# K cache loaded as whole 32 KB rows with four heads side by side, and one ring of three tiles for wq, K, V and wo

## The chip, the cores and the metric

The kernel runs on one core of one Trainium2 chip. A core has TensorE (PE, matmuls; its weight loads are shown apart as PEld), VectorE (DVE), ScalarE (ACT), GpSimd (POOL) and SyncE (SP), which here only issues transfers. Sixteen DMA engines move data between the chip's main memory (DRAM in the names) and the on-chip memory SBUF, which has 128 partitions; matmuls write to PSUM. The metric is the device time of one execution in microseconds (us).

## The reference

One token passes through an attention branch and a gated feed-forward branch; a sigmoid gate mixes both. All arrays are bf16, and of the cache of 65536 positions only the last 4096 are used.

```python
# D=512, Hq=32 query heads, Hkv=8 cached heads, Dh=128, W=4096, F=1792
q = (x @ wq).reshape(B, Sq, Hq, Dh).transpose(0, 2, 1, 3)      # wq: 512 x 4096
k = repeat(k_cache[:, :, Sk - W:, :], 4, axis=1)
v = repeat(v_cache[:, :, Sk - W:, :], 4, axis=1)
p = softmax(einsum("bhqd,bhkd->bhqk", q, k) * Dh ** -0.5)
a = einsum("bhqk,bhkd->bhqd", p, v).reshape(B, Sq, Hq * Dh) @ wo   # wo: 4096 x 512
b = (sigmoid(x @ w_gate) * (x @ w_up)) @ w_down
g = sigmoid((x * gate_w).sum(-1))
out = g * a + (1 - g) * b
```

## The kernel before, in words

**Loads.** All large loads are issued on SP, in this order: wq (4 MB, line 76), K as two loads of four heads each (4 MB each, lines 83 to 86), w_gate and w_up (1.75 MB each, lines 88 to 91), V as one load of heads 0 to 3, one of heads 4 and 5, and one each of heads 6 and 7 (lines 96 to 107) with w_down in two halves between them, and wo in six pieces (lines 109 to 112, bounds in `WO_SPLIT`). In the K and V loads partition p gets 32 consecutive positions of each head, which is one run of 8 KB per head and partition (`load_blocks`, line 78).

**Buffers.** A tile pool hands out a fixed number of buffers per tag; a new tile waits until the tile that had the buffer is no longer used. Pool `big` has one buffer of 32 KB per partition: wq, and after it wo. Pool `blk` has two of 32 KB: the two K tiles `kn`, and after them the two V tiles `vv`. Pool `ktp` has four of 8 KB: `q_sb`, `qtT`, then the transposed K tiles `kT`. So V's first load waits on SP until heads 0 to 3 of K have been transposed, V's second until heads 4 to 7 have been, and wo until wq has been read.

**The query (lines 153 to 173).** For each k of 4, eight matmuls (four chunks c of wq by two halves of 512 columns) make 1024 columns of x @ wq, equal in all partitions; ACT copies them to `q_sb`, DVE transposes them in 32 x 32 blocks of 4-byte words into `qtT`, and after the fourth k eight DVE copies scatter the query into `qbig`, whose slices are the stationary operands of the scores.

**The scores S (lines 176 to 188).** For each head g, DVE transposes the head's K tile in 32 x 32 blocks of 4-byte words, that is, of bf16 pairs (line 180). A pair holds two of the head's dimensions, so the dimension index is split into dhi (which half), a part that lies on the partitions, and t (which of the pair). Four pairs (dhi, t) by two halves of the positions give 8 matmuls of 512 columns per head, all of which accumulate in the two PSUM banks of `S_ps` (line 185). Neighbouring columns of the moving operand lie 2 elements apart, which is 4 bytes:

```python
        k_v = kT[:].rearrange("p (kb dhi s t) -> p kb dhi s t", kb=KB, dhi=2, s=32)
                                     rhs=k_v[:, hb * 16:(hb + 1) * 16, dhi, :, t],
```

**From S to the output.** DVE takes the row maxima of S (`pm`, line 192), PE and DVE bring them together per head (lines 194 to 199), ACT computes exp with the row sums (line 205), and DVE transposes the result into `eT` (line 207). PE meanwhile makes the gate and up products `gu_ps` (line 215), and DVE and ACT turn them into `hT` (lines 221 to 231). Then come the row sums per head (`rb_ps`, line 237), the products with V (`pv_ps`, line 267, two groups of four heads), their selection and scaling (lines 272 to 279), a transpose to `oY` (lines 283 to 287), and two matmuls of one row per 128 rows of w_down and of wo (`add_row`, line 248), all summed in `a_ps`. DVE and ACT copy one half of it each, and two transfers write the output.

**What sets the order.** Each engine runs its instructions in one order, fixed when the kernel is built; across engines, they wait for one another on semaphores. A transfer on SP that waits for a buffer holds back the transfers behind it in the order of issue.

Of the kernel before, what the change touches and what calls it, by code (L numbers as in the profile page):

```python
# [9 lines left out]
AF = mybir.ActivationFunctionType  # L10
ALU = mybir.AluOpType
AX = mybir.AxisListType
BF16 = mybir.dt.bfloat16
F32 = mybir.dt.float32
# [3 lines left out]
def kernel(  # L18
# [14 lines left out]
    nc = tc.nc  # L33

    P = 128
    D = A_x.shape[-1]
    DC = D // P
    Hkv = A_k_cache.shape[1]
    Sk = A_k_cache.shape[2]
    DH = A_k_cache.shape[3]  # L40
    HQ = A_wq.shape[1] // DH
    REP = HQ // Hkv
    W = min(4096, max(256, Sk // 4))
    KB = W // P
    SBASE = Sk - W
# [8 lines left out]
    scale = float(DH) ** -0.5  # L54
# [1 line left out]
    NJ_A = NJ // 2  # L56

    const = ctx.enter_context(tc.tile_pool(name="const", bufs=1))
    big = ctx.enter_context(tc.tile_pool(name="big", bufs=1))
    blk = ctx.enter_context(tc.tile_pool(name="blk", bufs=2))  # L60
    w14 = ctx.enter_context(tc.tile_pool(name="w14", bufs=3))
    ktp = ctx.enter_context(tc.tile_pool(name="ktp", bufs=4))
    work = ctx.enter_context(tc.tile_pool(name="work", bufs=1))
    ps_big = ctx.enter_context(tc.tile_pool(name="ps_big", bufs=2, space=bass.MemoryType.PSUM))
    ps_S = ctx.enter_context(tc.tile_pool(name="ps_S", bufs=1, space=bass.MemoryType.PSUM))
# [7 lines left out]
    dq = nc.sync  # L73
    wq_sb = big.tile([P, DC, HQ * DH], BF16, name="wq_sb", tag="big")
    wq_v = A_wq.rearrange("(p c) n -> p c n", c=DC)
    dq.dma_start(wq_sb[:], wq_v)

    def load_blocks(t, cache, g0, n, at=0):
        dq.dma_start(t[:, at:at + n, :, :],
                     cache[0, g0:g0 + n, SBASE:SBASE + W, :].rearrange("g (p kb) d -> p g kb d", kb=KB))  # L80

    kn = []
    for i in range(2):
        t = blk.tile([P, 4, KB, P], BF16, name="kn", tag="blk")
        load_blocks(t, A_k_cache, 4 * i, 4)
        kn += [t[:, j] for j in range(4)]

    wg_sb = w14.tile([P, DC, F], BF16, name="wg_sb", tag="w14")
    dq.dma_start(wg_sb[:], B_w_gate.rearrange("(p c) f -> p c f", c=DC))
# [5 lines left out]

    vv = []
    for i in range(2):
        t = blk.tile([P, 4, KB, P], BF16, name="vv", tag="blk")
        vv += [t[:, j] for j in range(4)]
        if i == 0:  # L100
            load_blocks(t, A_v_cache, 0, 4)
        else:
            load_blocks(t, A_v_cache, 4, 2)
            load_blocks(t, A_v_cache, 6, 1, at=2)
            dq.dma_start(wd_sb[:, 0:NJ_A, :], wd_v[:, 0:NJ_A, :])
            load_blocks(t, A_v_cache, 7, 1, at=3)
            dq.dma_start(wd_sb[:, NJ_A:NJ, :], wd_v[:, NJ_A:NJ, :])
# [24 lines left out]
    for c in range(DC):  # L132
        nc.tensor.matmul(xt_ps[:, c:c + 1], lhsT=xr[:, 0, c:D:DC], rhs=ident[0:1, 0:1],  # L133
                         start=True, stop=True, skip_group_check=True)
# [15 lines left out]
    nc.vector.tensor_scalar(gg[:, 1:2], gg[:, 0:1], -1.0, 1.0, op0=ALU.mult, op1=ALU.add)  # L150


    q_sb = ktp.tile([P, HQ * DH], BF16, name="q_sb", tag="kt")
    qtT = ktp.tile([P, HQ * DH], BF16, name="qtT", tag="kt")
    for k in range(4):
        q_ps = ps_big.tile([P, 2, 512], F32, name="q_ps", tag="b")
        for c in range(DC):
            for hb in range(2):
                n0 = k * 1024 + hb * 512
                nc.tensor.matmul(q_ps[:, hb, :], lhsT=xT[:, c:c + 1].to_broadcast([P, P]),  # L160
                                 rhs=wq_sb[:, c, n0:n0 + 512], start=(c == 0), stop=(c == DC - 1))
        nc.scalar.copy(q_sb[:, k * 1024:(k + 1) * 1024], q_ps[:].rearrange("p a b -> p (a b)"))  # L162
        nc.vector.transpose(qtT[:].bitcast(F32)[:, k * 512:(k + 1) * 512],  # L163
                            q_sb[:].bitcast(F32)[:, k * 512:(k + 1) * 512])

    q_src = qtT[:].rearrange("p (g hh dhi r t) -> p g hh dhi r t", g=Hkv, hh=REP, dhi=2, r=32)
    q_dst = qbig[:].rearrange("p (g y) -> p g y", y=2 * GS)[:, :, 0:4 * P] \
        .rearrange("p g (dhi c t) -> p g c dhi t", dhi=2, t=2)
    for qd in range(4):
# [3 lines left out]
    q_st = qbig[:, 0:Hkv * 4 * P].rearrange("p (g dhi c t) -> p g dhi c t", g=Hkv, dhi=2, t=2)  # L173


    S_ps = ps_S.tile([P, 2, 512], F32, name="S_ps", tag="S")
    S_f = S_ps[:].rearrange("p a b -> p (a b)")
    for g in range(Hkv):
        kT = ktp.tile([P, KB * P], BF16, name="kT", tag="kt")
        nc.vector.transpose(kT[:].bitcast(F32), kn[g].rearrange("p k d -> p (k d)").bitcast(F32))  # L180
        k_v = kT[:].rearrange("p (kb dhi s t) -> p kb dhi s t", kb=KB, dhi=2, s=32)
        for dhi in range(2):
            for t in range(2):
                for hb in range(2):
                    nc.tensor.matmul(S_ps[:, hb, :], lhsT=q_st[:, g, dhi, :, t],  # L185
                                     rhs=k_v[:, hb * 16:(hb + 1) * 16, dhi, :, t],
                                     start=(g == 0 and dhi == 0 and t == 0),
                                     stop=(g == Hkv - 1 and dhi == 1 and t == 1))


    pm = work.tile([P, 1], F32, name="pm")
# [8 lines left out]
                     start=True, stop=True)  # L200
    nb = work.tile([P, 1], F32, name="nb")
    nc.scalar.mul(nb[:], mb_ps[:], -scale)
    e_sb = work.tile([P, W // 4], BF16, name="e_sb")
    rs = work.tile([P, 1], F32, name="rs")
    nc.scalar.activation(e_sb[:], S_f, AF.Exp, bias=nb[:], scale=scale, accum_out=rs[:])
    eT = work.tile([P, Hkv, KB, REP], BF16, name="eT")
    nc.vector.transpose(eT[:].rearrange("p g k h -> p k g h"),
                        e_sb[:].rearrange("p (k g h) -> p k g h", g=Hkv, h=REP))
# [3 lines left out]
    for c in range(DC):  # L212
        for j in range(4):
            for w, wsb in enumerate((wg_sb, wu_sb)):
                nc.tensor.matmul(gu_ps[32 * j:32 * j + 32, w, 0:FQ],  # L215
                                 lhsT=xT[:, c:c + 1].to_broadcast([P, 32]),
                                 rhs=wsb[:, c, j * FQ:(j + 1) * FQ], start=(c == 0), stop=(c == DC - 1))
# [39 lines left out]
    for b in range(2):  # L257
        last = b == 1
        pv_ps = ps_big.tile([P, 4, P], F32, name="pv_ps", tag="b")
        for gq in range(4):  # L260
            g = 4 * b + gq
            if g == Hkv - 1:
                down(0, NJ_A)
            for m in range(KB // 4):
# [3 lines left out]
                                 lhsT=eT[:, g, 4 * m:4 * m + wj, :].rearrange("p k h -> p (k h)"),  # L268
                                 rhs=vv[g][:, 4 * m:4 * m + 4, :],
                                 start=(m == 0), stop=(m == KB // 4 - 1), skip_group_check=True)  # L270
# [5 lines left out]
        for j in range(4):  # L276
            nc.tensor.matmul(o_ps[:], lhsT=pv_sb[:, j, :], rhs=sel_v[:, j, :, :],  # L277
                             start=(j == 0), stop=(j == 3))
# [49 lines left out]
```

## Time and profile before

| What | Value |
|---|---|
| Median of 3 runs | 81.83 us (81.78 to 82.42) |
| Profiled execution: its time | 81.94 us |
| Profiled execution: span from the first to the last instruction | 80.2 us |
| Moved by DMA | 30.71 MB in 3738 packets, mean 383 GB/s over the span |
| PE, PEld, DVE, ACT, POOL busy | 48.7, 22.8, 35.1, 8.8, 5.0 us |
| Matmuls of S (line 185), 64 | 17.0 us busy, from 27.84 to 45.1 us |
| Transposes of K (line 180), 8 | 17.7 us busy, from 25.48 to 43.14 us |
| wq lands | 13.07 us |
| Last wo matmul ends | 77.44 us |

Times in the profile count from the start of the span. The span is shorter than the time of the execution by what lies around it. Each of the 40 digits in a row of slices is the busy share of 2.0 us in tenths; PEclk is the clock that TensorE was granted, in tenths of full speed. A line of the timeline gives the start, the length, the engine and line, what is written from what, how many such instructions were merged, and in brackets the idle time before and what ended it. Durations of matmuls overlap, so their pace is read from the starts of neighbours or from a group's length over its count.

### The profile page before, as it was taken

The numbers are of one execution on the slowest core, as the hardware profiler recorded it, in microseconds if no ns is written. First come the engines' busy times: TensorE is split into PE (matmuls) and PEld (weight loads), VectorE is DVE, ScalarE is ACT, GpSimd is POOL, SyncE is SP. The second block draws the span as 40 slices with busy tenths as digits, with TensorE's granted clock in tenths as the row PEclk, the third lists the DMA queues.
The fourth block names the chain that finished last, engine by engine and source line by source line (L and its number), as shares of the span: only waits on it lengthen the run. The fifth ranks groups of instructions, "written<-read, shape, count | busy, mean of one in ns | idle before, by whom it ended". The sixth has DMA issues, their size and how long they took to land.

```text
span 80.2 us, 774 instructions
## 1 busy us (share of the span) xinstructions
PE 48.7 (61%) x313; PEld 22.8 (28%) x313; DVE 35.1 (44%) x43; ACT 8.8 (11%) x13; POOL 5.0 (6%) x10
## 2 busy tenths in 40 slices
PE   0010204999800199999998970007999699678560
PEld 0000201344200032344443430004333545356330
DVE  0000720014359999999995449998000000020020
ACT  2400000055630000000000035000000200200010
POOL 7970000000000000000000000000000000000000
PEclk9999999999999655699999999555558999999999
DMA  7679988999999999999999999999999999999400
GB/s 180 262 343 524 425 360 372 442 425 425 425 425 417 433 409 445 419 451 422 422 397 437 401 433 413 429 413 425 413 418 436 416 426 417 425 409 399 182 8 1
DMA packets 3738, 30.71 MB, mean 383 GB/s; under 512 B 276, under 2 KB 408, under 8 KB 920
## 3 DMA queue, kind: packets, MB, share of 16 engines
q1 hardware_dynamic: 3730, 30.67, 92.3%
q8 instruction: 2, 0.03, 0.2%
q10 hardware_dynamic: 6, 0.00, 0.0%
HBM read 30.67 MB, written 0.00 MB: 383 GB/s over the span
## 4 chain that ended last, share of the span: by engine, by line
DMA 57%; DVE 23%; PE 12%; issue 3%; ACT 1%; DVEq 0%
DMA wo_sb<-in_A_wo_dram 23%; DVE kT L180 20%; DMA vv<-in_A_v_cache_dram 18%; DMA wq_sb<-in_A_wq_dram 15%; PE q_ps L160 11%; DVE qbig L172 2%; PE a_ps L248 2%; ACT q_sb L162 1%; DVE qtT L163 1%; DVE res L294 1%; DVEq L180 0%; DVEq L172 0%
## 5 line engine op out<-in xcount | busy, mean ns | idle before, releaser
L185 PE MATMUL S_ps<-kT,qbig 128*128 128x512 bf16 x64 | 17.0, 429 | 6.4 <-DVE kT L180 6.4
L180 DVE STREAM_TRANSPOSE kT<-kn 128x2048 f32<-128x2048 f32 x8 | 17.7, 2274 | 0.0
L267 PE MATMUL pv_ps<-vv,eT 128*16 128x512 bf16 (+1 forms) x64 | 12.0, 465 | 0.0
L185 PEld LDWEIGHTS <-qbig 128*128 128x128 bf16 x64 | 6.8, 106 | 16.5 <-issue 6.6
L160 PE MATMUL q_ps<-wq_sb,xT 128*128 128x512 bf16 x32 | 8.6, 437 | 3.2 <-DMA wq_sb<-in_A_wq_dram 3.2
L163 DVE STREAM_TRANSPOSE qtT<-q_sb 128x512 f32<-128x512 f32 x4 | 2.8, 711 | 10.0 <-ACT q_sb L162 10.0
L279 DVE TENSOR_TENSOR oT<-o_ps,rb 128x16 bf16<-128x16 f32 x2 | 0.3, 174 | 14.6 <-PE o_ps L277 14.6
L267 PEld LDWEIGHTS <-eT 128*16 128x16 bf16 (+1 forms) x64 | 4.5, 104 | 6.4 <-issue 3.6
L160 PEld LDWEIGHTS <-xT 128*128 128x128 bf16 x32 | 3.5, 109 | 7.9 <-issue 5.3
L162 ACT CAST q_sb<-q_ps 128x1024 bf16<-128x1024 f32 x4 | 4.0, 1012 | 8.6 <-PE q_ps L160 8.6
L248 PE MATMUL a_ps<-wo_sb,oY 128*1 128x256 bf16 x64 | 4.2, 272 | 1.2 <-DMA wo_sb<-in_A_wo_dram 1.2
L237 PE MATMUL rb_ps<-lsel,ones_f 128*128 128x32 f32 x2 | 0.6, 398 | 6.9 <-DVE lsel L235 6.9
L141 DVE TENSOR_TENSOR gpr<-xr 1x512 f32<-1x512 bf16 x1 | 0.7, 679 | 7.9 <-DMA xr<-in_gate_w_dram 7.9
L126 POOL MEMSET qbig<- 128x4160 bf16 x1 | 3.6, 3564 | 0.0
L248 PEld LDWEIGHTS <-oY 128*1 128x1 bf16 x64 | 2.9, 83 | 2.5 <-issue 1.7
L133 PE MATMUL xt_ps<-ident,xr 1*128 1x1 bf16 x4 | 0.3, 165 | 5.2 <-POOL ident L118 5.2
L272 ACT COPY pv_sb<-pv_ps 128x512 f32<-128x512 f32 x2 | 1.2, 585 | 19.1 <-PE pv_ps L267 19.1
L221 ACT ACTIVATE sge<-gu_ps 128x448 f32<-128x448 f32 x1 | 0.5, 543 | 24.6 <-PE gu_ps L215 24.6
L294 DVE CAST res<-a_ps 1x256 bf16<-1x256 f32 x1 | 0.4, 412 | 5.9 <-PE a_ps L248 5.9
L224 DVE RECIPROCAL sg<-sge 128x448 f32<-128x448 f32 x1 | 3.0, 2954 | 0.0
L144 PE MATMUL z_ps<-gsum,ones_f 1*128 1x1 f32 x2 | 0.6, 358 | 3.9 <-DVE gsum L142 3.9
L277 PE MATMUL o_ps<-identf,pv_sb 128*128 128x16 f32 x16 | 2.1, 265 | 1.4 <-ACT pv_sb L272 1.4
(49 smaller groups left out, 28.2 us busy)
## 6 DMA issues: line engine op xcount, KB each, us to landing
kn<-in_A_k_cache_dram SPq DMA_DIRECT2D x2, 4096.0 KB
wq_sb<-in_A_wq_dram SPq DMA_DIRECT2D x1, 4096.0 KB, 12.3
vv<-in_A_v_cache_dram SPq DMA_DIRECT2D x1, 4096.0 KB, 18.1
wo_sb<-in_A_wo_dram SPq DMA_DIRECT2D x3, 1024.0 KB, 22.7
vv<-in_A_v_cache_dram SPq DMA_DIRECT2D x1, 2048.0 KB
vv<-in_A_v_cache_dram SPq DMA_DIRECT2D x2, 1024.0 KB, 16.3
wg_sb<-in_B_w_gate_dram SPq DMA_DIRECT2D x1, 1792.0 KB, 35.0
wu_sb<-in_B_w_up_dram SPq DMA_DIRECT2D x1, 1792.0 KB, 32.5
```

Of the source, the lines that this page charges most:

```text
L126: nc.gpsimd.memset(qbig[:], 0.0)
L160: nc.tensor.matmul(q_ps[:, hb, :], lhsT=xT[:, c:c + 1].to_broadcast([P, P]), rhs=wq_sb[:, c, n0:n0 + 512], start=(c == 0), stop=(c == DC - 1))
L162: nc.scalar.copy(q_sb[:, k * 1024:(k + 1) * 1024], q_ps[:].rearrange("p a b -> p (a b)"))
L163: nc.vector.transpose(qtT[:].bitcast(F32)[:, k * 512:(k + 1) * 512], q_sb[:].bitcast(F32)[:, k * 512:(k + 1) * 512])
L172: nc.vector.tensor_copy(q_dst[rows, :, 32 * qd:32 * qd + REP, :, t], q_src[rows, :, :, :, 0, t])
L180: nc.vector.transpose(kT[:].bitcast(F32), kn[g].rearrange("p k d -> p (k d)").bitcast(F32))
L185: nc.tensor.matmul(S_ps[:, hb, :], lhsT=q_st[:, g, dhi, :, t], rhs=k_v[:, hb * 16:(hb + 1) * 16, dhi, :, t], start=(g == 0 and dhi == 0 an ...
L224: nc.vector.reciprocal(sg[:], sge[:])
L248: nc.tensor.matmul(a_ps[32 * i:32 * i + 1, i, 0:HN], lhsT=lhsT, rhs=rhs[:, i * HN:(i + 1) * HN], start=start, stop=stop)
L267: nc.tensor.matmul(pv_ps[32 * gq:32 * gq + mm, :, :], lhsT=eT[:, g, 4 * m:4 * m + wj, :].rearrange("p k h -> p (k h)"), rhs=vv[g][:, 4 * m ...
L277: nc.tensor.matmul(o_ps[:], lhsT=pv_sb[:, j, :], rhs=sel_v[:, j, :, :], start=(j == 0), stop=(j == 3))
L294: nc.vector.tensor_copy(res[0:1, :], a_ps[0:1, 0, 0:HN])
```

## The change

K is read so that partition p = 4r + g holds head g (of the four heads of the load) at 128 consecutive positions, one run of 32 KB; the four heads of a load are interleaved over the partitions. wq is loaded in two halves by chunks c. Pool `big` becomes a ring of three buffers of 32 KB which wq, K, K, V, V and wo take in turn, and pool `blk` is gone. Pool `ktp` has two buffers of 16 KB: `qq` (which holds `q_sb` and `qtT`), then four tiles `kT`, each filled by two transposes of the old size. In a transposed row, four heads j now stand side by side in each of eight groups s of a block, so a matmul takes one head's columns 8 elements apart, and it covers one half nb of the positions with all 512 columns. Exp writes its output in another order of indices so that everything after it stays as it was.

In the new order of instructions PE does, of the query's matmuls, those with c = 0, 1 of the first two k first, then those with c = 2, 3 of the same two, then the rest as before. On SP the first V load now waits for the query's matmuls on PE, the second for the transposes of the first K tile, and the first piece of wo for those of the second K tile.

```diff
-    big = ctx.enter_context(tc.tile_pool(name="big", bufs=1))
-    blk = ctx.enter_context(tc.tile_pool(name="blk", bufs=2))
+    big = ctx.enter_context(tc.tile_pool(name="big", bufs=3))
...
-    ktp = ctx.enter_context(tc.tile_pool(name="ktp", bufs=4))
+    ktp = ctx.enter_context(tc.tile_pool(name="ktp", bufs=2))
...
-    dq.dma_start(wq_sb[:], wq_v)
+    for i in range(2):
+        dq.dma_start(wq_sb[:, 2 * i:2 * i + 2, :], wq_v[:, 2 * i:2 * i + 2, :])
...
     for i in range(2):
-        t = blk.tile([P, 4, KB, P], BF16, name="kn", tag="blk")
-        load_blocks(t, A_k_cache, 4 * i, 4)
-        kn += [t[:, j] for j in range(4)]
+        t = big.tile([P, P, P], BF16, name="kn", tag="big")
+        dq.dma_start(t[:].rearrange("p n d -> p (n d)"),
+                     A_k_cache[0, 4 * i:4 * i + 4, SBASE:SBASE + W, :].rearrange("g (r n) d -> r g (n d)", r=32))
+        kn.append(t)
...
-        t = blk.tile([P, 4, KB, P], BF16, name="vv", tag="blk")
+        t = big.tile([P, 4, KB, P], BF16, name="vv", tag="big")
...
-    q_sb = ktp.tile([P, HQ * DH], BF16, name="q_sb", tag="kt")
-    qtT = ktp.tile([P, HQ * DH], BF16, name="qtT", tag="kt")
+    qq = ktp.tile([P, 2, HQ * DH], BF16, name="qq", tag="kt")
+    q_sb = qq[:, 0, :]
+    qtT = qq[:, 1, :]
...
-    for g in range(Hkv):
-        kT = ktp.tile([P, KB * P], BF16, name="kT", tag="kt")
-        nc.vector.transpose(kT[:].bitcast(F32), kn[g].rearrange("p k d -> p (k d)").bitcast(F32))
-        k_v = kT[:].rearrange("p (kb dhi s t) -> p kb dhi s t", kb=KB, dhi=2, s=32)
-        for dhi in range(2):
-            for t in range(2):
-                for hb in range(2):
-                    nc.tensor.matmul(S_ps[:, hb, :], lhsT=q_st[:, g, dhi, :, t],
-                                     rhs=k_v[:, hb * 16:(hb + 1) * 16, dhi, :, t],
-                                     start=(g == 0 and dhi == 0 and t == 0),
-                                     stop=(g == Hkv - 1 and dhi == 1 and t == 1))
+    NH = P // 2
+    for i in range(2):
+        for nb in range(2):
+            kT = ktp.tile([P, NH * P], BF16, name="kT", tag="kt")
+            for u in range(2):
+                w = NH * P // 2
+                nc.vector.transpose(kT[:, u * w:(u + 1) * w].bitcast(F32),
+                                    kn[i][:].rearrange("p n d -> p (n d)")
+                                    [:, (2 * nb + u) * w:(2 * nb + u + 1) * w].bitcast(F32))
+            k_v = kT[:].rearrange("p (n dhi s j t) -> p n dhi s j t", n=NH, dhi=2, s=8, j=4)
+            for j in range(4):
+                for dhi in range(2):
+                    for t in range(2):
+                        nc.tensor.matmul(S_ps[:, nb, :], lhsT=q_st[:, 4 * i + j, dhi, :, t],
+                                         rhs=k_v[:, :, dhi, :, j, t],
+                                         start=(i == 0 and j == 0 and dhi == 0 and t == 0),
+                                         stop=(i == 1 and j == 3 and dhi == 1 and t == 1))
...
-    nc.scalar.activation(e_sb[:], S_f, AF.Exp, bias=nb[:], scale=scale, accum_out=rs[:])
+    nc.scalar.activation(e_sb[:].rearrange("p (k i h) -> p h k i", k=KB, i=8),
+                         S_f.rearrange("p (h k i) -> p h k i", h=4, k=KB), AF.Exp, bias=nb[:], scale=scale, accum_out=rs[:])
```

More of the change, by code (lines that the diff above doesn't have):

```diff
@@ L162 @@
         nc.scalar.copy(q_sb[:, k * 1024:(k + 1) * 1024], q_ps[:].rearrange("p a b -> p (a b)"))
-        nc.vector.transpose(qtT[:].bitcast(F32)[:, k * 512:(k + 1) * 512],
-                            q_sb[:].bitcast(F32)[:, k * 512:(k + 1) * 512])
-    q_src = qtT[:].rearrange("p (g hh dhi r t) -> p g hh dhi r t", g=Hkv, hh=REP, dhi=2, r=32)
+        nc.vector.transpose(qtT.bitcast(F32)[:, k * 512:(k + 1) * 512],
+                            q_sb.bitcast(F32)[:, k * 512:(k + 1) * 512])
+    q_src = qtT.rearrange("p (g hh dhi r t) -> p g hh dhi r t", g=Hkv, hh=REP, dhi=2, r=32)
     q_dst = qbig[:].rearrange("p (g y) -> p g y", y=2 * GS)[:, :, 0:4 * P] \
```

## The prediction

> **What bounds the kernel now.** I read the page's parts 1 and 2 first (busy time by engine; 40 slices of 2 us), since the kernel moves 30.67 MB and computes little:
>
> ```profile
> PE 48.7 (61%) x313; PEld 22.8 (28%) x313; DVE 35.1 (44%) x43; ACT 8.8 (11%) x13; POOL 5.0 (6%) x10
> ...
> PEclk9999999999999655699999999555558999999999
> DMA  7679988999999999999999999999999999999400
> GB/s 180 262 343 524 425 360 372 442 425 425 425 425 417 433 409 445 419 451 422 422 397 437 401 433 413 429 413 425 413 418 436 416 426 417 425 409 399 182 8 1
> ```
>
> The DMA row is at 9 from slice 7 (14 us) to slice 36 (74 us): transfers never stop, at some 422 GB/s, while no engine is busy over 61%. So the last byte of wo sets the end, provided the computation is ready for it. The timeline shows how ready it is (start, length, instruction; idle time before it in brackets):
>
> ```profile
> 25.48 17.66 DVE L180 STREAM_TRANSPOSE kT<-kn 128x2048 f32<-128x2048 f32 x8
> ...
> 28.23 0.14 PEld L185 LDWEIGHTS <-qbig 128*128 128x128 bf16 x1 [0.28 <-issue]
> 28.65 0.14 PEld L185 LDWEIGHTS <-qbig 128*128 128x128 bf16 x1 [0.28 <-issue]
> ...
> 33.35 9.29 PEld L185 LDWEIGHTS <-qbig 128*128 128x128 bf16 x43 [0.28 <-issue]
> ...
> 43.19 1.91 PE L185 MATMUL S_ps<-kT,qbig 128*128 128x512 bf16 x8 [0.27 <-DVE kT L180]
> ...
> 45.14 1.23 DVE L192 TENSOR_REDUCE pm<-S_ps 128x1 f32<-128x1024 f32 x1 [2.00 <-PE S_ps L185]
> ...
> 55.22 7.15 PE L267 MATMUL pv_ps<-vv,eT 128*32 128x512 bf16 x32
> ...
> 72.03 1.91 PE L248 MATMUL a_ps<-wo_sb,oY 128*1 128x256 bf16 x32
> 74.63 1.04 PE L248 MATMUL a_ps<-wo_sb,oY 128*1 128x256 bf16 x16 [0.68 <-DMA wo_sb<-in_A_wo_dram]
> ...
> 76.19 1.25 PE L248 MATMUL a_ps<-wo_sb,oY 128*1 128x256 bf16 x16 [0.52 <-DMA wo_sb<-in_A_wo_dram]
> ```
>
> Three readings. First, the last two groups wait for wo: the end is the DMA's, and the computation has little in hand. Its 48 matmuls on the first 24 blocks need about 47 x 0.053 + 0.27 = 2.8 us (0.053 is (1.91 - 0.27)/31, the pace of the first 32), so without DMA waits they would be over at 74.8, and the last 16 start at 76.19: **slack 1.3 us**. Second, from the start of pm (45.14) to the first wo matmul (72.03) there are 26.9 us in which PE, DVE and ACT hand work to one another; V's loads delay none of it (the PV group shows no idle time). So a later end of the S matmuls moves all of it. Third, the S phase is paced by DVE: eight transposes, one each 2.19 us, without a gap. PE follows: one load of weights per matmul, 0.43 us apart at first (28.23 to 28.65, PEclk 5 and 6) and 9.29/43 = 0.216 us once the clock is full, so 8 matmuls (1.73) fit under one transpose (2.19).
>
> Then the waits of the SP queue, since tiles change owners (total, times, longest):
>
> ```profile
> SPq L79 <- DVE kT L180: 19.7, 2, 11.4
> ...
> SPq L79 <- DMA kn<-in_A_k_cache_dram: 11.0, 1, 11.0
> ```
>
> SP ended issuing wu at 11.97, so the first K tile landed at 11.97 + 11.0 = 22.97, and V's loads were issued at 34.4 and 43.2, when K had been transposed. These waits cost nothing: at 34.4 the view by windows (GB/s in each stretch of 2 us) sums to 13.6 MB moved of 16.25 MB queued, 6 us of cover.
>
> [...] S's moving operand has a 4-byte step now[...] at 0.216 us per 512 columns, no slower than the unit-step q matmuls once warm. [...]
>
> **The change, part by part.**
>
> *wq in two loads.* One more issue on SP (0.40 us), so K is queued 0.4 us later, behind 10 us of wq: hidden. The first half should land near 8 us (2.1 MB; the windows sum to 1.6 MB at 6 us, 2.6 MB at 8). Now q starts at 13.11, after the whole of wq. Per the instruction order PE does c = 0,1 of the first two k first: 8 matmuls, 3.4 us at half clock, from about 9.9 (xT was ready at 9.64), which fill the time until the rest lands at 13.1. There remain 24 x 0.216 = 5.2 us, the ACT copy and DVE transpose of the last k (1.01 + 0.71) and eight qbig copies (1.80): DVE free near 22.3 in place of 25.4. Then K's landing, 23.0, is the wait. So transposes start at about 23.1, **2.4 us earlier**.
>
> *K as 128 rows of 32 KB.* The packets fall from 1024 to 256, the bytes stay. The trace has 14 KB (w_gate, w_up) and 8 KB packets at 423 and 420 to 430 GB/s: no dependence, so I take 0. [...]
>
> *The ring of three.* V's first tile takes wq's place and is issued when q is done (about 19, not 34.4); its second takes the first K tile's (about 32, not 43.2); wo takes the second K tile's, issued last, when the eighth transpose ends. Even at 46 us, some 18.6 of the 26.5 MB ahead of wo have moved: 18 us of cover. Cost 0. Queued behind a waiting V load on SP are only later loads.
>
> *kT in two tiles of twice the size.* Still eight transposes at 2.19 us, but PE starts after two, and the last group is 16 matmuls. Tiles: the fifth transpose needs the first 16 matmuls done, the seventh the next 16. At 0.216 us: transposes 1 and 2 end at 23.1 + 4.5 = 27.6; 16 matmuls[...] take 5.1 to 6.8, so the fifth transpose starts at 32.9 to 34.4; four take 8.8, and 16 matmuls and the drain 3.6: S ends at **45.3 to 46.8, against 45.1 now**, within the slack.
>
> *The step in S's moving operand.* Within a row, the 32 x 32 transposes now leave four heads side by side: for one head, dhi and t, neighbouring columns are (j, t) = 8 bf16 = **16 bytes** apart[...]; it was 4 bytes. Nothing in the trace shows this. Bounds: 0.216 us (no price) and no upper end that I can derive; the nearest measured value is 0.43[...]. I take that estimate, **0.427**. Then PE is the bound: it starts at 27.65 and runs 64 x 0.427 = 27.3 us without a gap (third group ready at 39.2, needed at 41.3; fourth at 46.0, needed at 48.1). S ends at 55.1, **10.0 us later**.
>
> *Exp with a strided output.* It reads PSUM in order and writes at an 8-byte step[...]: 0. It took 1.11 us; at twice that it would still be hidden, since eT waits on DVE until 51.3 behind the 2.95 us reciprocal, 2 us after exp.
>
> **Sum.** Start of wo's matmuls 55.1 + 26.9 = 82.0; 64 of them without DMA waits 63 x 0.053 + 0.27 = 3.6: 85.6. Now they end at 77.44, so +8.2; the span becomes 88.4. The profiled execution took 81.94 at a span of 80.2, 1.74 more: 90.1; the median is 0.1 below that execution, so **90.0 us**.
>
> **Rivals.**
>
> *The 16-byte step is free.* [...] S ends at 45.3 to 46.8, wo's first 48 matmuls 29.7 us later at 75.0 to 76.5, against 76.19: the end stays the DMA's, **81.8 us** (81.3 to 82.6). This is the other side. It decides by the pace of the S matmuls: with the last 48 paced by PE from about 34 to 46.4, the border is near 0.25 us.
>
> *Free, and the start of the loads improves.* In the first 14 us the windows sum to 4.94 MB, 11.6 us' worth at 425 GB/s: 2.4 us lost, some 1.2 of it before the first bytes. If 16 and 32 KB packets win back 1 us, 80.8. Against it: wq already came in 32 KB packets while this was lost.
>
> *Another price.* At 0.32 us S ends near 50.0, giving 84.9; at four times 0.216, S takes 55 us, over 115 us.
>
> **How the numbers follow.** Half rate 0.60; a price between 0.25 and 0.40, 0.09; a heavier one 0.05; free with the end unmoved 0.18, of which 0.04 is slower by over 1% (a cold PV phase or a late K); free with a gain 0.08. About 1% is what a measurement of this kernel tells from none. Slower 0.60 + 0.09 + 0.05 + 0.04 = 0.78, same 0.14, faster 0.08. The likeliest case alone has 88.5 to 92.0: [...] transposes may start only at 25.5 (+2.4, if q is not earlier). Slow cases below 92 hold only 0.7, so the range reaches down to the free case: 81.5 to 92.0, leaving out the gain, the heavy price and some tails.
>
> **What would show it.** Right: the S group at about 0.43 us per matmul while PEclk reads 9; DVE waiting for PE at the fifth and seventh transposes; S ending near 55; no wait for wo by its matmuls; the DMA row falling to 0 near 76 with 10 us of span left. Separately: a first transpose near 23, V's first issue near 19. Wrong: a 0.216 us pace in the S group, and a wo wait ahead of the last matmuls.

## The result, and the profile after

The changed kernel takes **119.0 us** (median of 4 runs, 118.36 to 119.67) against 81.89 us (81.78 to 82.42) for the kernel before: a ratio of **1.451 (1.439 to 1.464)**. Its profiled execution took 118.46 us at a span of 116.3. A ratio here and below compares only the fast executions of both kernels, those within 1.5% of the fastest of the same kernel. The direction was forecast; the size was not, and the time lies far above the range.

The slices of the page (here of 2.9 us each):

```profile
PE   0029794006999999999999999999970089797890
...
PEclk9999999955555555555555555555555556999999
DMA  4999998998999999999999999600000000000000
GB/s 102 423 417 423 440 530 372 440 462 361 435 434 434 399 423 426 420 423 423 416 426 416 421 417 410 263 3 0 0 0 0 0 0 0 0 0 6 0 0 0
```

The DMA row ends in slice 25, near 75 us; in the kernel before it ended only some 4 us ahead of the span. PE is busy from slice 10 to slice 29 (the first slice is 0), with PEclk at 5 throughout. The groups of the page (busy time, mean ns of one, then the idle time before):

```profile
L194 PE MATMUL S_ps<-kT,qbig 128*128 128x512 bf16 x64 | 55.1, 1036 | 8.5 <-DVE kT L187 8.5
L187 DVE STREAM_TRANSPOSE kT<-kn 128x2048 f32<-128x2048 f32 x8 | 17.9, 2285 | 19.1 <-PE S_ps L194 18.9
```

The 64 matmuls of S take 55.1 us, 17.0 before, and DVE, which paced them, now waits 18.9 us for PE. The timeline has the rest:

```profile
22.77 8.89 DVE L187 STREAM_TRANSPOSE kT<-kn 128x2048 f32<-128x2048 f32 x4 [0.28 <-DMA kn<-in_A_k_cache_dram]
27.32 55.15 PE L194 MATMUL S_ps<-kT,qbig 128*128 128x512 bf16 x64 [8.53 <-DVE kT L187]
...
28.17 0.12 PEld L194 LDWEIGHTS <-qbig 128*128 128x128 bf16 x1 [0.74 <-issue]
29.03 0.12 PEld L194 LDWEIGHTS <-qbig 128*128 128x128 bf16 x1 [0.73 <-issue]
...
82.51 1.22 DVE L201 TENSOR_REDUCE pm<-S_ps 128x1 f32<-128x1024 f32 x1 [22.99 <-PE S_ps L194]
...
93.87 6.41 PE L277 MATMUL pv_ps<-vv,eT 128*32 128x512 bf16 x32
...
109.94 3.66 PE L258 MATMUL a_ps<-wo_sb,oY 128*1 128x256 bf16 x64
113.63 0.41 DVE L304 CAST res<-a_ps 1x256 bf16<-1x256 f32 x1 [4.16 <-PE a_ps L258]
```

One weight load per matmul, 0.86 us apart (28.17, 29.03). The same pace holds late in S, when DMA moves nothing (0 GB/s from 76 to 82 us) and DVE is idle, so it is not traffic of theirs that slows the matmuls:

```profile
78.86 0.12 PEld L194 LDWEIGHTS <-qbig 128*128 128x128 bf16 x1 [0.74 <-issue]
79.72 0.12 PEld L194 LDWEIGHTS <-qbig 128*128 128x128 bf16 x1 [0.74 <-issue]
```

The final copy of the kernel before, for comparison:

```profile
77.46 0.41 DVE L294 CAST res<-a_ps 1x256 bf16<-1x256 f32 x1 [5.90 <-PE a_ps L248]
```

Where the time went: pm starts at 82.51 in place of 45.14, +37.4. From pm to the first wo matmul it is 27.4 us (26.9 before), +0.5. The wo matmuls no longer wait for loads: 3.7 us from their start to the final copy (5.4 before), -1.7. Sum +36.2, and the final copy starts at 113.63 in place of 77.46, which is 36.2 later.

### The profile page after: what moved, and what is told of

The parts are those of the page before. It is cut to its first block, busy times and chain, and to the rows that moved or that the text cites. A ratio compares the mean times of both kernels' runs of the same rounds, so it can differ in the third digit from the quotient of the medians.

```text
span 116.3 us, 774 instructions
## 1 busy us (share of the span) xinstructions
PE 87.5 (75%) x313; PEld 24.3 (21%) x313; DVE 35.3 (30%) x43; ACT 10.1 (9%) x13; POOL 5.0 (4%) x10
## 4 chain that ended last, share of the span: by engine, by line
PE 66%; DMA 18%; DVE 9%; ACT 1%; issue 1%; SPq 1%
PE S_ps L194 47%; DMA kn<-in_A_k_cache_dram 18%; PE pv_ps L277 9%; PE a_ps L258 4%; DVE kT L187 4%; PE gu_ps L225 3%; DVE sg L234 3%; PE o_ps L287 2%; DVE h_sb L236 2%; ACT pv_sb L282 1%; SPq L76 1%; PE rb_ps L247 1%; ACT sge L231 0%; DVE sge L232 0%; DVE res L304 0%
## 5 line engine op out<-in xcount | busy, mean ns | idle before, releaser
L194 PE MATMUL S_ps<-kT,qbig 128*128 128x512 bf16 x64 | 55.1, 1036 | 8.5 <-DVE kT L187 8.5
L187 DVE STREAM_TRANSPOSE kT<-kn 128x2048 f32<-128x2048 f32 x8 | 17.9, 2285 | 19.1 <-PE S_ps L194 18.9
L194 PEld LDWEIGHTS <-qbig 128*128 128x128 bf16 x64 | 7.9, 123 | 54.5 <-issue 50.4
L277 PE MATMUL pv_ps<-vv,eT 128*16 128x512 bf16 (+1 forms) x64 | 11.3, 437 | 0.0
L163 PE MATMUL q_ps<-wq_sb,xT 128*128 128x512 bf16 x32 | 9.1, 442 | 1.1 <-DMA wq_sb<-in_A_wq_dram 0.9
L201 DVE TENSOR_REDUCE pm<-S_ps 128x1 f32<-128x1024 f32 x1 | 1.2, 1223 | 23.0 <-PE S_ps L194 23.0
L166 DVE STREAM_TRANSPOSE qq<-qq 128x512 f32<-128x512 f32 x4 | 2.8, 711 | 8.3 <-ACT qq L165 8.3
L165 ACT CAST qq<-q_ps 128x1024 bf16<-128x1024 f32 x4 | 4.0, 1014 | 7.0 <-PE q_ps L163 7.0
L258 PE MATMUL a_ps<-wo_sb,oY 128*1 128x256 bf16 x64 | 3.7, 273 | 0.0
L225 PE MATMUL gu_ps<-wu_sb,xT 128*32 128x448 bf16 x16 | 2.8, 581 | 0.0
L225 PE MATMUL gu_ps<-wg_sb,xT 128*32 128x448 bf16 x16 | 2.8, 575 | 0.0
```

The source lines that it names most:

```text
L166: nc.vector.transpose(qtT.bitcast(F32)[:, k * 512:(k + 1) * 512], q_sb.bitcast(F32)[:, k * 512:(k + 1) * 512])
L187: nc.vector.transpose(kT[:, u * w:(u + 1) * w].bitcast(F32), kn[i][:].rearrange("p n d -> p (n d)") [:, (2 * nb + u) * w:(2 * nb + u + 1) ...
L194: nc.tensor.matmul(S_ps[:, nb, :], lhsT=q_st[:, 4 * i + j, dhi, :, t], rhs=k_v[:, :, dhi, :, j, t], start=(i == 0 and j == 0 and dhi == 0 ...
L225: nc.tensor.matmul(gu_ps[32 * j:32 * j + 32, w, 0:FQ], lhsT=xT[:, c:c + 1].to_broadcast([P, 32]), rhs=wsb[:, c, j * FQ:(j + 1) * FQ], star ...
L258: nc.tensor.matmul(a_ps[32 * i:32 * i + 1, i, 0:HN], lhsT=lhsT, rhs=rhs[:, i * HN:(i + 1) * HN], start=start, stop=stop)
L277: nc.tensor.matmul(pv_ps[32 * gq:32 * gq + mm, :, :], lhsT=eT[:, g, 4 * m:4 * m + wj, :].rearrange("p k h -> p (k h)"), rhs=vv[g][:, 4 * m ...
```

## The experiments

Two questions were open. Is it the step of the operand, or something else in the change? And why is the price twice the estimate: does a column cost twice a dense one at whatever clock is granted, with a clock that happens to be half, or does it cost a fixed time? The runs with one step alone (8, 16 and 32 bytes) and the two warm runs were executed once each; their main evidence is the pace of the S matmuls in the trace.

**The step taken away, everything else kept.** The transposes write each head's pairs side by side, so that the matmuls read runs of 8 pairs at a 4-byte step.

```diff
-                nc.vector.transpose(kT[:, u * w:(u + 1) * w].bitcast(F32),
+                nc.vector.transpose(kT[:, u * w:(u + 1) * w].bitcast(F32)
+                                    .rearrange("p (m j s) -> p m s j", j=4, s=8),
...
-            k_v = kT[:].rearrange("p (n dhi s j t) -> p n dhi s j t", n=NH, dhi=2, s=8, j=4)
+            k_v = kT[:].rearrange("p (n dhi j s t) -> p n dhi j s t", n=NH, dhi=2, j=4, s=8)
```

> All of the change is kept, but the eight transposes write each head's pairs side by side, so that the moving operand of the S matmuls again has a 4-byte step (runs of 32 bytes). Theory: the step alone made S slow. Then the S matmuls run at 0.216 us each with a full clock (0.43 while the clock is half), S ends at 45 to 47 us, and the time is 80.5 to 82 us, about that of the kernel before or a little less, since the loads start better. Rival: the ring, the larger K tiles or the new layout of K in SBUF slow the S matmuls; then they stay near 0.86 us and the time stays above 110 us.

Measured: 92.67 us, ratio 1.125 (1.116 to 1.133). Groups and timeline:

```profile
L196 PE MATMUL S_ps<-kT,qbig 128*128 128x512 bf16 x64 | 20.3, 484 | 18.2 <-DVE kT L187 18.2
L187 DVE STREAM_TRANSPOSE kT<-kn 128x2048 f32<-128x2048 f32 x8 | 29.2, 3776 | 0.3 <-DMA kn<-in_A_k_cache_dram 0.3
```

```profile
37.45 3.34 PEld L196 LDWEIGHTS <-qbig 128*128 128x128 bf16 x16 [1.49 <-issue]
```

PE is back to its old pace once the clock is full: 16 matmuls in 3.34 us, 0.21 each, at a PEclk of 1.00 from 37 to 41 us. So the ring, the tiles and the layout of K do not slow S; the step does. But the time did not come back to 82 as expected. The price has moved to the writer: DVE now writes 4-byte words 32 bytes apart, and a transpose takes 29.2/8 = 3.65 us in place of 17.9/8 = 2.24. PE waits 18.2 us for DVE.

**The step alone, on the kernel before.** Only which columns each S matmul takes is changed; their number, their size, the tiles and the loads stay. S adds other columns of K than the reference does.

```diff
-        k_v = kT[:].rearrange("p (kb dhi s t) -> p kb dhi s t", kb=KB, dhi=2, s=32)
+        k_v = kT[:].rearrange("p (m j t) -> p m j t", j=4, t=2)
...
-                                     rhs=k_v[:, hb * 16:(hb + 1) * 16, dhi, :, t],
+                                     rhs=k_v[:, 0:512, j, t],
```

> The kernel before with one thing changed: the S matmuls take columns 8 elements (16 bytes) apart, in the same number and size. It adds other columns of K into S than the reference does, so S is not the scores. Theory (the step alone): 0.86 us per matmul, PEclk at half all through S, S ends near 27.8 + 55 = 83 us, time 118 to 121 us. Rival (the step costs only together with the new tiles and loads): 0.22 to 0.43 us per matmul, time 82 to 92 us.

Measured: 124.84 us. The S group:

```profile
L187 PE MATMUL S_ps<-kT,qbig 128*128 128x512 bf16 x64 | 57.8, 1079 | 6.1 <-DVE kT L180 6.1
```

57.8/64 = 0.90 us: the step alone does it, even a little more than in the change. The time is 4 us above what was expected: 2.7 us of that is the pace (57.8 against 55.1), and 1.0 us is that S started later (28.88, in the kernel before 27.84).

**Is it the clock?** Dense matmuls between the query and S keep PE busy, so that S starts with a full clock (PEclk 1.00 from 20 to 32 us).

```diff
+    w_ps = ps_big.tile([P, 2, 512], F32, name="w_ps", tag="b")
+    for i in range(34):
+        nc.tensor.matmul(w_ps[:, 0, :], lhsT=q_sb[:, 3968:4096], rhs=q_sb[:, 3584:4096], start=True, stop=True)
```

> The changed kernel with 34 added dense matmuls of 512 columns (their result is not used) between the query and S, which keep PE busy until S starts. Theory A: a 16-byte step costs two PE cycles per column, whatever the clock, and the clock is half in S [...]. Then the first S matmuls take 0.43 us with a full clock, the clock falls after some us and the pace becomes 0.86; time 114 to 118 us. Theory B: a 16-byte step costs a fixed 1.68 ns per column in the memory; then the first S matmuls take 0.86 us with a full clock too, and the time stays 118 to 120 us.

Measured: 118.32 us. Timeline, then the windows (PE, PEld, DVE, ACT and POOL busy, granted clock, DMA share, GB/s):

```profile
28.07 0.12 PEld L198 LDWEIGHTS <-qbig 128*128 128x128 bf16 x1 [0.74 <-issue]
28.93 0.12 PEld L198 LDWEIGHTS <-qbig 128*128 128x128 bf16 x1 [0.74 <-issue]
29.79 0.12 PEld L198 LDWEIGHTS <-qbig 128*128 128x128 bf16 x1 [0.74 <-issue]
```

```profile
28.00:30.00 2.00, 2.00 (x4) 0.35 (x3) 2.00 (x2) 0.00 (x0) 0.00 (x0) 1.00 1.14 492
...
34.00:36.00 2.00, 2.00 (x4) 0.37 (x3) 0.00 (x0) 0.00 (x0) 0.00 (x0) 0.50 0.99 423
```

From 28 to 30 us the granted clock is 1.00, and the matmuls still come 0.86 us apart; at 34 us the clock is 0.50 and the pace is the same (loads at 34.08 and 34.94). At both clocks the price is the same time, 0.859/512 = 1.68 ns per column. Theory A falls: the half clock does not cause the slow pace, it goes along with it. Where in the chip the time is spent was not shown.

**The same with the clock held.** A dense matmul of 512 columns is added ahead of each S matmul.

```diff
+                        m = 4096 + 512 * ((4 * j + 2 * dhi + t) % 8)
+                        nc.tensor.matmul(w_ps[:, 0, :], lhsT=q_st[:, 4 * i + j, dhi, :, t],
+                                         rhs=kT[:, m:m + 512], start=True, stop=True)
```

> As the run with the warm start, and ahead of each of the 64 S matmuls one added dense matmul of 512 columns from the same transposed K tile (its result is not used). Theory A (two cycles per column[...]): a pair takes 0.43 + 0.22 = 0.65 us with a full clock, S takes 41 us and ends near 69, the time is 103 to 108 us, so that more work makes it faster; if the clock is half all the same, a pair takes 0.86 + 0.43 = 1.29 us and the time is near 145 us. Theory B (fixed 1.68 ns per column): a pair takes 0.86 + 0.22 = 1.08 us, S takes 69 us, the time is near 132 us.

Measured: 133.34 us, the 132 of theory B. From its timeline:

```profile
29.98 1.02 PE L201 MATMUL S_ps<-kT,qbig 128*128 128x512 bf16 x1
...
31.06 1.02 PE L201 MATMUL S_ps<-kT,qbig 128*128 128x512 bf16 x1
```

A pair takes 1.08 us (29.98 to 31.06), that is 0.86 + 0.22, while the clock stays at 1.00 from 28 to 100 us (slices of 3.3 us):

```profile
PEclk9999999999999999999999999999999555899779
```

So with a full clock all through S the strided matmuls are as slow as before, 0.86 us.

**How the price depends on the step.** 8 bytes on the kernel before, as in the run with 16 bytes but with j=2 and two halves of 512 columns; S again adds other columns than the reference.

> The kernel before with one thing changed: the S matmuls take columns 4 elements (8 bytes) apart, in the same number and size. It adds other columns of K into S than the reference does, so S is not the scores. Theory 1 [...]: 8 bytes are free, 0.216 us per matmul with a full clock, S still paced by DVE, time 81.5 to 82.5 us. Theory 2 (the price grows with the step from 4 bytes on): 0.43 us per matmul or so with a full clock too, S takes 27 us and ends near 55, time 89 to 92 us.

Measured: 93.16 us, 1 us above the second case, as S started at 29.13, not 27.84. The timeline shows 0.45 us at half and at full clock alike (PEclk 0.50 from 26 to 32 us, 1.00 from 34 us on; slices of 2.3 us):

```profile
PEclk9999999999965589999999999998555599999999
...
29.57 0.12 PEld L187 LDWEIGHTS <-qbig 128*128 128x128 bf16 x1 [0.33 <-issue]
30.02 0.12 PEld L187 LDWEIGHTS <-qbig 128*128 128x128 bf16 x1 [0.33 <-issue]
...
38.16 0.12 PEld L187 LDWEIGHTS <-qbig 128*128 128x128 bf16 x1 [0.34 <-issue]
38.61 0.12 PEld L187 LDWEIGHTS <-qbig 128*128 128x128 bf16 x1 [0.34 <-issue]
```

So the 8-byte step is not free, 0.45 us against 0.216: theory 1 falls. And 32 bytes, in the changed kernel (columns taken 16 elements apart, other columns than the reference's):

```diff
-            k_v = kT[:].rearrange("p (n dhi s j t) -> p n dhi s j t", n=NH, dhi=2, s=8, j=4)
+            k_v = kT[:].rearrange("p (x j t) -> p x j t", j=8, t=2)
...
-                                         rhs=k_v[:, :, dhi, :, j, t],
+                                     rhs=k_v[:, :, j, t],
```

> The changed kernel with the S matmuls taking columns 16 elements (32 bytes) apart instead of 8, in the same number and size. It adds other columns of K into S than the reference does, so S is not the scores. Theory 1 [...]: 0.86 to 0.90 us per matmul as at 16 bytes, time 118 to 122 us. Theory 2 (the price is for the bytes spanned, 9.5 per ns): 1.72 us per matmul, S takes 110 us, time near 174 us.

Measured: 121.76 us. The S group:

```profile
L193 PE MATMUL S_ps<-kT,qbig 128*128 128x512 bf16 x64 | 58.9, 1098 | 8.5 <-DVE kT L187 8.5
```

58.9/64 = 0.92 us: hardly more than the 0.86 to 0.90 at 16 bytes, so it is not the bytes spanned that cost, and theory 2 falls. The four steps together, per matmul of 512 columns:

| Step | Columns per 16 bytes | us | ns per 16 bytes touched |
|---|---|---|---|
| 4 bytes | 4 | 0.216 (PE's own pace) | 1.7 or less |
| 8 bytes | 2 | 0.45 (0.435 below) | 1.8 (1.7) |
| 16 bytes | 1 | 0.86 to 0.90 | 1.7 to 1.8 |
| 32 bytes | 1 | 0.92 | 1.8 |

The last column divides the time by the number of 16-byte stretches of a partition's row that hold a column: at most 1.7 to 1.8 ns each in all four rows. At 4 bytes it cannot be told from PE's pace with columns side by side (0.22 us for the added matmul of a pair, above): four columns take 4 x 0.216/512 = 1.7 ns. The runs themselves give the 16 bytes: counted in stretches of 8 bytes, a step of 16 would cost no more than one of 8 (measured 0.86 to 0.90 against 0.45), and in stretches of 32 a step of 32 would cost twice that of 16 (0.92 against 0.86 to 0.90). This is a pattern of the times; what makes it was not shown.

**The loads: what the other parts of the change are worth.** wq in halves on the kernel before (the diff's wq lines alone), and the same with the ring of three 32 KB tiles:

> The kernel before with wq loaded in two halves, nothing else. Theory 1 (smaller wq packets make the loads start better, and the end is the loads' end): the last wo group starts 0.5 to 1 us earlier, time 80.9 to 81.5 us; the query ends 3 us earlier, which is worth nothing by itself. Theory 2 (the better start comes from K's rows): time 81.8 to 82.0 us.

> The kernel before with wq in two halves and the ring of three 32 KB tiles, K loaded and S computed as before. Theory 1 (the ring costs and brings nothing, since loads never ran out): the same time as with the halves alone, within 0.3 us. Theory 2 (the earlier issue of V and the later issue of wo change the flow of the loads): a difference of over 0.5 us either way.

Measured: 82.06 us, ratio 1.003 (1.001 to 1.005), and 82.18 us, ratio 1.003 (1.001 to 1.006). Neither gains. With the halves alone the last wo matmuls still wait until 76.16, as before (76.19):

```profile
76.16 1.22 PE L249 MATMUL a_ps<-wo_sb,oY 128*1 128x256 bf16 x16 [0.52 <-DMA wo_sb<-in_A_wo_dram]
```

In the changed kernel the loads did end earlier, by some 0.5 us. The windows from 74 to 75 us, of the changed kernel and then of the kernel before (the last figure is GB/s):

```profile
74.00:75.00 1.00, 1.00 (x2) 0.12 (x1) 0.00 (x0) 0.00 (x0) 0.00 (x0) 0.50 0.61 216
...
74.00:75.00 1.00, 0.37 (x8) 0.30 (x9) 0.00 (x0) 0.00 (x0) 0.00 (x0) 1.00 0.94 349
```

From 74 us on the changed kernel still moves 0.24 MB and the kernel before 0.44: 0.2 MB less, 0.5 us at 422 GB/s. Up to 12 us both had moved the same (4.18 and 4.19 MB), so the lead is not won in the first bytes but while K is loaded. By 74 us the four traced kernels with K in rows of 32 KB whose loads never paused had moved 30.45 to 30.46 MB, the kernel before 30.27, the one with the halves 30.25 and the one with the ring too 30.28. So the gain belongs to K's long rows, which my prediction put at 0.

**A way to keep part of it.** Two heads side by side in place of four: rows of 16 KB, an 8-byte step, four loads of K, and the transposed tiles and those of the query as in the kernel before.

```diff
-        t = big.tile([P, P, P], BF16, name="kn", tag="big")
+        t = big.tile([P, 2, 64, P], BF16, name="kn", tag="big")
...
-            k_v = kT[:].rearrange("p (n dhi s j t) -> p n dhi s j t", n=NH, dhi=2, s=8, j=4)
+                k_v = kT[:].rearrange("p (n dhi s j t) -> p n dhi s j t", n=KB, dhi=2, s=16, j=2)
```

> The changed kernel with two heads side by side instead of four: K in rows of 16 KB, four loads, transposed tiles of the old size, and an 8-byte step in the S matmuls. If 8 bytes are free: S is paced by DVE and ends at 41 to 44 us, and the loads set the end; with their better start the time is 80.3 to 81.5 us. If 8 bytes cost twice the time of 4: S ends near 52 us, time 86 to 91 us.

Measured: 83.97 us, ratio 1.024 (1.021 to 1.028). From the trace, which is of an execution of 86.00 us:

```profile
L192 PE MATMUL S_ps<-kT,qbig 128*128 128x512 bf16 x64 | 27.8, 610 | 6.6 <-DVE qbig L176 6.6
```

```profile
55.22 1.22 DVE L199 TENSOR_REDUCE pm<-S_ps 128x1 f32<-128x1024 f32 x1 [11.53 <-PE S_ps L192]
...
61.69 0.61 PE L275 MATMUL pv_ps<-vv,eT 128*32 128x512 bf16 x1
```

S takes 27.8 us (0.435 per matmul, twice the time at 4 bytes), as the second case said, and pm starts at 55.2; the time is still lower than that case because the order of instructions changed too: the part of the gate's work that stood ahead of the products with V on DVE came after them, and PV (the products with V) began 6.5 us after pm, not 10.1. Then the eight copies into `qbig` (the scatter of the query) were moved to ACT (`nc.scalar.copy` for `nc.vector.tensor_copy`), to start S earlier:

> The two-head kernel with the eight small copies into qbig on ACT in place of DVE, so that S can start when the query is scattered, near 23 us, and not at 27.3. S still takes 64 x 0.435 = 27.8 us, so it ends near 51 in place of 55. If PE's chain after S (28.7 us to the end of the span) is kept, the span is 79.5 and the loads, which end near 75 here, set the end: 80.8 to 81.5 us, up to 1% less than the kernel before. If S starts no earlier (DVE or the landing of K holds it), 83.5 to 84.5 us.

Measured: in the traced execution (83.97 us) S started at 25.9, not 23, because the scatter takes 3.06 us on ACT and DVE put a K transpose ahead of the query's last. The 23 runs spread from 81.34 to 85.63 us with a median of 82.72, 1% above the 81.93 of the kernel before; the ratio is 0.997 (0.994 to 1.000). So no version here beats the kernel before.

## Why the prediction was wrong

**The step that failed** is the price of the 16-byte step: "I take that estimate, 0.427". The place was right: S's moving operand, PE as the bound, DVE waiting at the fifth and seventh transposes (9.6 and 9.2 us), no wait for wo, a DMA row that ends near 75. The term was mis-sized: a matmul took 0.859 us, and 64 x (0.859 - 0.427) = 27.6 us of the 29 us by which the time was missed. The error was to take for the price the pace of the 4-byte step at half clock: twelve weight loads from 28.23 to 33.35 us in the kernel before, 0.427 us each, 0.427/512 = 0.83 ns per column, since nothing else was measured. That a 16-byte step would cost this was my estimate. The warm runs show a time of 1.68 ns per column, at a PEclk of 1.00 and of 0.50 alike. The prediction also named a PEclk of 9 during S as a sign of being right; it read 5, which by the warm runs is without effect on this pace (0.86 us at 1.00 and at 0.50). One sum was off without effect: the slack of 1.3 us is 76.19 - 74.8 = 1.4.

**The rival "four times 0.216"** gave over 115 us and was right to within a few us, with a chance of 0.05. It stood there without a reason; the runs supply one: the time doubled from 4 to 8 bytes (0.216 us, then 0.435 to 0.45) and again from 8 to 16 bytes (0.86 to 0.90). The prediction itself said that the upper end of this price could not be derived, and then ended its range at one estimate of it.

**wq in halves**: transposes were to start at 23.1 and started at 22.77, after K landed. Right, and worth nothing, as argued, since the loads set the end of the kernel before.

**K's rows**: put at 0; the loads ended about 0.5 us earlier. It was hidden here behind PE.

**The ring**: V's first load was issued at 18.8, wo's first at 59.55, with no gap in the DMA row; its cost of 0 was right, and the run with ring and halves agrees (82.18 us, with the halves alone 82.06).

**Exp**: put at 0, which was my estimate. It went from 1.11 to 2.52 us in the changed kernel, above the bound of twice; it was hidden as argued, for eT began at 89.95, about when the reciprocal ended (87.08 + 2.95 = 90.03).

**The case that the step is free** would have needed S at 0.216; the run with the step taken away gave that pace but did not reach its time, because the reordering has a price on DVE (3.65 us per transpose, 2.24 in the changed kernel). That the first 16 matmuls would take 5.1 to 6.8 us was my estimate: 8 or all 16 of them at 0.427 us, the others at 0.216. In that run they took 6.04 us. The lower end of the likeliest case, 88.5 us, was my estimate too.

## What to carry to other kernels

When a new layout puts elements that one instruction reads in sequence farther apart, count how many of them fall into 16 bytes before counting anything else: here a matmul of 512 columns took 0.216 us with four, 0.435 to 0.45 with two and 0.86 to 0.90 with one. Moving the gather to the instruction that writes the tile moved a price to that engine: 3.65 us per transpose on DVE in place of 2.24. And when a price has no measured upper end, let the range say so, above all if it is multiplied by the 64 instructions that then form the critical path.

## What the runs showed of the hardware that was not expected

- During the S matmuls at a 16-byte step PEclk fell although PE counts as busy all the time: in the run with the warm start from 1.00 (28 to 32 us) over 0.78 (32 to 34) to 0.50 (from 34 us on). In the run with the 8-byte step it rose from 0.50 (26 to 32 us) to 1.00 and stayed there (34 to 56), and with one dense matmul for each 16-byte one it stayed 1.00 (28 to 100). After S the changed kernel still had a PEclk of 0.50 (82 to 86 us; 1.00 from 45 to 47 in the kernel before), and its gate and up matmuls started in groups 0.37 us apart in place of 0.19. This cost about 1.3 us: from pm to the activation on the gate's product it took 3.6 us, 2.3 before. Of this 0.5 us was left at the first wo matmul, as the first 32 products with V took 6.4 us, 7.2 before.
- The price on DVE's writes looks alike: a transpose of 2048 words took 3.65 us with words 32 bytes apart (1.8 ns per word), 2.24 with words side by side. Whether the cause is the same is not shown.
- ACT's exp of 1024 columns took 1.11 us with its output in order, 1.42 at a 4-byte step (two heads) and 2.52 at an 8-byte step (four heads). At the 1.7 ns of the matmuls per 16 bytes touched, the last would come to 512 x 1.7 = 0.9 us, which does not account for it.
- An operand of eight columns and then a jump was a little faster than one of 512 columns at an even 16-byte step (0.86 against 0.90 us). Why stays open.
- SP needed 6.7 us to issue the load of w_gate behind K's 1024 packets, and 0.6 us behind 256; nothing waited for it.
